# A third group of 256 tokens, fourteen whole seven-product groups, sums of g in three operations, and another order of the later steps

## The chip, the cores and the metric

The kernel runs on one core of a Trainium2 chip. The metric is the device time of one execution in microseconds (us). A core has five engines that each work through a queue of their own in order: TensorE (PE, with its weight loads PEld), VectorE (DVE), ScalarE (ACT), GpSimd (POOL) and SyncE (SP, which issues most DMAs).

## The reference, cut to what matters

```
a = softmax(phi, axis=2)                       # (8, 8, 576, 32)
k_m, v_m = a^T k, a^T v                        # (8, 8, 32, 64)
attn = softmax(scale * q k_m^T)                # (8, 8, 576, 32)
x = (attn v_m) as (4608, 512)                  # 8 batches of S = 576 tokens
h = x @ w_in                                   # w_in (512, 2048)
g = max(0.01 * h, h)
out = g @ w_out                                # w_out (2048, 512)
```

The inputs of the first part are float32, the weights come as 64-bit floats and are brought to float32 on the chip. What costs is the second part, two large products over 4608 tokens.

## The kernel before, in words

**Folding.** Attention ends in scores a of 32 memories per head, 256 values per token. v_m is folded into w_in once per batch b and quarter j of the 2048 hidden columns (`fold_products`, L1235, a step `W{b}{j}.p`; ACT writes the high half of the folded weights, L1268, steps `h0 h1`; DVE the low half, L1274, steps `l0 l1`). So h is a product over 256 values instead of 512.

**Precision.** Every factor is a pair of float16 halves, and a product is three matmuls: high by high, low by high, high by low.

**The older groups.** Tokens are taken in groups. Groups G = 0, 1 and 2 have 384 tokens each (batches 0 and 1, 1152 tokens). G = 0 is done in float32 while the weights still arrive. G = 1 and 2 go by units m of 256 hidden columns, eight a group: `P{m}.i` the up product (L1328, `up_products`, six matmuls for each 128 hidden columns), `V` the leaky activation on ACT (L1335), `C` the high half of g (`hi_old`, L1345, a copy on DVE), `L` the low half (`lo_old`, L1349, DVE), `O{m}.i` the down product (L1415): for each 128 hidden columns three tiles of 128 tokens, three matmuls of 512 columns each. `Z{G}.t` scales a tile on ACT and sends it with four DMAs on SP.

**The later groups.** Batches 2 to 7 (3456 tokens) go in 14 groups of 256 tokens, G = 3 to 16; the 14th has 128 tokens. A group has four steps k, one per quarter j (k = 0 to 55). `p{k}.i` is an up product of 128 hidden columns (L1457, `up_late`): six matmuls of 256 columns, or six and six of the two parts where a group crosses from one batch into the next. Two such products share one PSUM bank, a half each. `v{k}.i` is the activation (ACT, L1473). For a whole group the down product saves one product in eight: two tiles of tokens by two halves of the 512 output columns by two halves of the hidden columns need eight block products, and sums and differences of blocks make it seven, as Strassen and Winograd do. `s{k}` makes four sums of g blocks of 256 columns (`add_g`, L1494, four DVE operations), `c{k}.h` the high halves (ACT, L1498), `l{k}.h` the low halves (DVE, L1502), and `d{k}.n`, n = 0 to 6, the products (L1525, `down_late`): each six matmuls of 256 columns, into one half of four accumulator banks (one of its own, p1, and three pairs). The sums of w_out blocks are made once (`add_up`, L454). When a group's four k are done, `x{G}.p` copies p1 (ACT, L1535), `x{G}.0` to `x{G}.3` add the banks up (DVE, L1538, L1540, L1543, L1545), `z{G}.t` scales and sends. The 14th group, of one tile, has no blocks to add: its `d{k}.n`, n = 0 to 7, are plain products (`down_tile`, L1560, three matmuls of 256 columns each, 96 in all), and `store_half` (L1392 to L1403) sends the two halves of its tile.

**What sets the order.** Nothing is scheduled by the compiler: `OPENING` and `LATER` list some 2150 step names, and each engine takes its instructions in the order in which the steps stand there. The framework sets the semaphores: a step waits for what it reads, for the readers of what it overwrites, and a new accumulator takes a PSUM bank when one has been read out.

Of the kernel before, what the change touches and what calls it, by code (L numbers as in the profile page):

```python
# [1720 lines left out]
```

## Time and profile before

| what | value |
|---|---|
| median of 3 runs | 646.2 us (645.8 to 647.45) |
| the profiled execution's own time | 645.63 us |
| its span, first to last instruction | 643.9 us |
| granted TensorE clock | 1.000 of full speed |
| PE / DVE / ACT busy | 634.0 / 512.9 / 394.2 us |
| matmuls recorded | 7149 |

The profiled execution lies 0.57 us below the median of the runs. Busy time of an engine is the union of its instructions. A matmul's recorded duration contains its way through the array, so consecutive ones overlap: what a matmul costs in a row of them is the distance from one to the next, which the chain of waits gives where it lists a run of matmuls with its length and count.

### The profile page before, as it was taken

To read this page: it belongs to the slowest core of one execution; us is meant where nothing else is said; L and a number is where in the kernel's file an instruction comes from. 1 tells how busy PE (TensorE), PEld (TensorE's weight loads), DVE (VectorE), ACT (ScalarE), POOL (GpSimd) and SP (SyncE) were. 2 spreads that over 40 slices of the span, in tenths; PEclk is the share of its full clock that TensorE was granted. 3 is DMA by queue.
4 is the path that set the end of the run, shared out by engine and by line. 5 is a ranking of instruction groups with operands and counts; after the bars stand their busy time and mean duration, and the time that the engine had idled before them with its cause. 6 is when DMAs were issued, how large, how long until landed. Compare 5 with 4: busy or idle time off the path is not lost.

```text
span 643.9 us, 16869 instructions
## 1 busy us (share of the span) xinstructions
PE 634.0 (98%) x7149; PEld 481.7 (75%) x7149; DVE 512.9 (80%) x861; ACT 394.2 (61%) x683; POOL 30.0 (5%) x46
## 2 busy tenths in 40 slices
PE   8999999999999999999999999999999999999997
PEld 4544455665546788888888888887888888889896
DVE  5776899998987899899779865799887897574641
ACT  3898987764553556477556655656574576565553
POOL 0000121000010001002000010000010001000000
PEclk9999999999999999999999999999999999999999
DMA  9998732214502645501271001164114101010102
GB/s 324 337 380 275 247 110 50 83 21 91 198 10 33 133 152 84 180 32 42 33 193 70 13 22 43 23 124 148 35 27 82 26 19 33 3 34 1 35 2 50
DMA packets 85403, 61.14 MB, mean 95 GB/s; under 512 B 61648, under 2 KB 68560, under 8 KB 85328
## 3 DMA queue, kind: packets, MB, share of 16 engines
q1 hardware_dynamic: 84848, 59.64, 32.6%
q8 instruction: 56, 0.92, 0.6%
q10 hardware_dynamic: 480, 0.43, 0.2%
q14 instruction: 19, 0.16, 0.1%
HBM read 50.59 MB, written 9.45 MB: 93 GB/s over the span
## 4 chain that ended last, share of the span: by engine, by line
PE 93%; DVE 2%; DMA 2%; ACT 1%; SPq 1%; issue 1%; POOL 0%; DVEq 0%; ACTq 0%; POOLq 0%
PE po L1525 31%; PE ph L1457 22%; PE po L1415 15%; PE ph L1328 8%; PE ph L1525 5%; PE pa L1235 4%; PE pa L788 3%; PE po L1560 1%; DMA arena<-in_moe_w_out_dram 1%; PE po L1623 1%; PE pa L1038 1%; SPq L615 1%; DMA arena<-in_q_dram 0%; ACT wi L424 0%; PE pa L357 0%
## 5 line engine op out<-in xcount | busy, mean ns | idle before, releaser
L1525 PEld LDWEIGHTS <-arena 128*128 128x128 f16 x2184 | 210.2, 98 | 32.9 <-issue 10.0
L1473 ACT ACTIVATE wi<-ph,g_sc 128x256 f32<-128x256 f32 (+1 forms) x224 | 98.8, 464 | 162.0 <-PE ph L1457 153.9
L1457 PE MATMUL ph<-a,w_mem 128*128 128x256 f16 (+3 forms) x1440 | 144.8, 246 | 0.0
L1457 PEld LDWEIGHTS <-w_mem 128*128 128x128 f16 x1440 | 114.7, 98 | 13.6 <-issue 2.9
L1525 PE MATMUL po<-arena 128*128 128x256 f16 x936 | 122.0, 273 | 0.0
L1525 PE MATMUL po<-wo,arena 128*128 128x256 f16 x936 | 122.0, 273 | 0.0
L1415 PE MATMUL po<-wo,arena 128*128 128x512 f16 (+1 forms) x384 | 110.3, 433 | 0.0
L1502 DVE TENSOR_TENSOR arena<-arena 128x1024 f16<-128x1024 f32 x52 | 63.5, 1221 | 21.3 <-ACT arena L1498 21.2
L1502 DVE TENSOR_TENSOR arena<-wi,arena 128x768 f16<-128x768 f32 (+1 forms) x60 | 54.6, 910 | 10.1 <-ACT arena L1498 10.1
L1494 DVE TENSOR_TENSOR arena<-wi 128x256 f32<-128x256 f32 x104 | 40.4, 429 | 25.9 <-ACT wi L1473 25.3
L1498 ACT CAST arena<-arena 128x1024 f16<-128x1024 f32 x52 | 54.4, 1046 | 8.0 <-DVE arena L1494 7.7
L1328 PE MATMUL ph<-a,w_mem 128*128 128x192 f16 (+2 forms) x304 | 52.1, 317 | 0.0
L1415 PEld LDWEIGHTS <-arena 128*128 128x128 f16 x288 | 27.9, 98 | 29.6 <-issue 0.6
L1498 ACT CAST arena<-wi 128x768 f16<-128x768 f32 (+1 forms) x60 | 46.5, 776 | 1.5
L1494 DVE TENSOR_TENSOR arena<-wi,arena 128x256 f32<-128x256 f32 x104 | 45.6, 439 | 1.8
L1525 PE MATMUL ph<-wo,arena 128*128 128x256 f16 x312 | 42.6, 273 | 1.0 <-DVE t L1114 1.0
L1200 POOL TENSOR_TENSOR a<-t,a 128x128 f16<-128x128 f32 (+3 forms) x17 | 21.7, 1296 | 445.0 <-ACT a L1195 445.0
L1415 PEld LDWEIGHTS po<-wo,arena 128*128 128x128 f32 x96 | 17.7, 190 | 20.4 <-issue 17.9
L1235 PE MATMUL pa<-wi,vT 64*32 64x512 f16 (+1 forms) x704 | 29.6, 420 | 0.1
L1328 PEld LDWEIGHTS <-w_mem 128*128 128x128 f16 x240 | 20.8, 98 | 10.6 <-issue 3.9
L1335 ACT ACTIVATE arena<-ph,g_sc 128x384 f32<-128x384 f32 x32 | 18.3, 579 | 16.1 <-PE ph L1328 15.8
L1268 ACT ACTIVATE w_mem<-pa 128x512 f16<-128x512 f32 x40 | 22.7, 596 | 8.4 <-PE pa L1235 7.4
(236 smaller groups left out, 759.6 us busy)
## 6 DMA issues: line engine op xcount, KB each, us to landing
out_dram<-obs SPq DMA_DIRECT2D x140, 64.0 KB, 1.7
arena<-in_q_dram SPq DMA_DIRECT2D x96, 72.0 KB, 2.8
arena<-in_moe_w_in_dram SPq DMA_DIRECT2D x12, 512.0 KB, 7.1
arena<-in_moe_w_out_dram SPq DMA_DIRECT2D x8, 768.0 KB, 7.9
arena<-in_k_dram SPq DMA_DIRECT2D x5, 1152.0 KB, 5.5
arena<-in_v_dram SPq DMA_DIRECT2D x5, 1152.0 KB, 9.1
arena<-in_phi_dram SPq DMA_DIRECT2D x7, 576.0 KB, 4.6
arena<-in_k_dram SPq DMA_DIRECT2D x8, 288.0 KB, 4.9
```

Of the source, the lines that this page charges most:

```text
L788: nc.tensor.matmul(var["pk"][g][hh * M:(hh + 1) * M, cs], ld["phi"][rows, hh, j, :], ld["kv", hh][rows, kinds[0]:kinds[-1] + 1, j, :], sta ...
L1200: nc.gpsimd.tensor_tensor(piece(lo, tb), piece(t2, tb), piece(hi, tb), ALU.subtract)
L1235: nc.tensor.matmul(pf[g][cols, :], lhs, rhs, start=(n == 0), stop=(n == len(passes) - 1), tile_position=(g * D, hh * M),)
L1268: nc.scalar.activation(tiles(halves(w16(b, j), g)[:, 0]), w(g), AF.Copy, scale=ws)
L1328: nc.tensor.matmul(ph[:, t0:t0 + n * SB], lhs, rhs, start=(m == 0), stop=(m == len(seq) - 1))
L1415: nc.tensor.matmul(po, lhs, rhs, start=(f == 0 and m == 0), stop=(f == NQ * NF - 1 and m == len(seq) - 1),)
L1457: nc.tensor.matmul(ph[:, t0:t0 + n], lhs, rhs, start=(m == 0), stop=(m == len(seq) - 1))
L1473: nc.scalar.activation(dst, ph, AF.Prelu, scale=g_sc2[:, j:j + 1], alpha=SLOPE)
L1494: nc.vector.tensor_tensor(gt[:, x], y, z, op)
L1498: nc.scalar.copy(dst[:, 0], src)
L1502: nc.vector.tensor_tensor(dst[:, 1], src, dst[:, 0], ALU.subtract)
L1525: nc.tensor.matmul(acc, g[:, x, s, u], rhs, start=(h == 0 and j == 0 and u == 0 and m == 0), stop=(j == NQ - 1 and u == 1 and m == 2), ski ...
```

## The change

G = 2 shrinks from 384 to 256 tokens (768 to 1023), its tile count from three to two, so that the later groups start at token 1024 instead of 1152 and 14 whole groups of 256 reach 4608. `down_tile` and `store_half` go; the last group is combined and sent by new steps `end.*`. G = 2 now reads a block of 192 tokens and a third of another (64), each as its own matmuls; the first later group reads 128 tokens of batch 1 and 128 of batch 2, so batch 1's folded weights serve it too. The signs of some sums are turned (w_out blocks and g blocks alike), which lets one operation of 512 columns make two of the four sums of g; the odd hidden tiles' activation produces the value with the other sign. The high half of g in the older groups moves from DVE to ACT. `LATER` and the last part of `OPENING` are new orders, found by a search that took a PSUM bank as one thing; steps of different k now stand much more mixed. `w_turn`, the turn of the buffers for folded weights, changes with it.

```diff
-    NG2 = -(-((B - 2) * S) // (2 * HT))
+    GL = 2 * P
+    X0 = 2 * S - P
+    NG2 = (B * S - X0) // (2 * HT)
...
-    w_turn = iter([4, 5, 0, 1, 4, 2, 0, 3] + [4, 0, 1, 2, 6, 3] * B)
+    w_turn = iter([4, 5, 0, 1, 4, 2, 0, 3] + [4, 0, 6, 1, 2, 3] * B)
...
+    def width(G):
+        return GL if G == G2 - 1 else GT
...
+        for b, tb, c0, t0, n in spans(G * GT, width(G)):
...
-        nc.vector.tensor_copy(g[:, 0], gf_old(u))
+        nc.scalar.copy(g[:, 0], gf_old(G, u))
...
-            pos[G] = [ps_o.tile([P, E], F32, name="po") for t in range(NT)]
-        for t in range(NT):
+            pos[G] = [ps_o.tile([P, E], F32, name="po") for t in range(width(G) // P)]
+        for t in range(width(G) // P):
...
-        for x, y, z, op in (
-            (0, gf[:, 0], gf[:, 2], ALU.add), (3, gf[:, 1], gf[:, 0], ALU.subtract),
-            (1, gf[:, 1], gt[:, 0], ALU.subtract), (2, gf[:, 3], gt[:, 1], ALU.add),
-        ):
-            nc.vector.tensor_tensor(gt[:, x], y, z, op)
+        two = gf[:, 0:1].broadcast_to([P, 2, 2 * P])
+        nc.vector.tensor_tensor(gt[:, 0:2], two, gf[:, 1:3], ALU.subtract)
+        nc.vector.tensor_tensor(gt[:, 2], gf[:, 1], gt[:, 1], ALU.subtract)
+        nc.vector.tensor_tensor(gt[:, 3], gf[:, 3], gt[:, 2], ALU.subtract)
...
+    def combine_last(n):
...
+        dst, psum, by, add = {
+            0: (o[:, 1], pair[0][:, 1], minus, o[:, 0]),
+            1: (o[:, 2], pair[1][:, 0], sc, o[:, 1]),
+            3: (o[:, 1], pair[2][:, 0], minus, o[:, 1]),
+            4: (o[:, 2], pair[2][:, 1], minus, o[:, 2]),
+            5: (o[:, 0], pair[0][:, 0], minus, o[:, 0]),
+        }.get(n, (None,) * 4)
...
+            nc.vector.scalar_tensor_tensor(dst, psum, by, add, ALU.mult, ALU.add)
+
+    def send_last(x, n):
...
+        for y, (b, x0) in enumerate(columns(G, t)):
+            eng = nc.scalar if y % 2 else nc.sync
+            eng.dma_start(
+                rows[b, x0 // 32, :, cs], obs[32 * y:32 * y + 32, x * EH:(x + n) * EH]
+            )
...
-        for n in range(7 if whole(G2 + m // NQ) else 2 * NF):
+        for n in range(7):
```

The turn from one group to the next in the old `LATER`, after k = 39 (group G = 12; the other turns look much like it):

```
v41.1 d39.1 x12.p d39.2
p41.2 x12.0 d39.3 v41.2 c40.1 d39.4 x12.1 p41.3 x12.2 d39.5 l40.0 v41.3 d39.6 c41.0 p42.0 x12.3
p42.1 l40.1 v42.0 d40.0 v42.1 z12.0 d40.1 s41 z12.1 d40.2 p42.2 l41.0 d40.3 v42.2 c41.1 d40.4 p42.3
```

Two places of the new `LATER` that the prediction reads, the end of the group whose last step is k = 47 and the fold of batch 6's last quarter, and its last lines:

```
v49.0 d46.5 d45.3 d45.4 v49.1 p49.2 c48.0 p49.3 d47.0 l48.0 v49.3 d46.3 v49.2 s48 c48.1 d47.6 p50.1
p50.0 x14.p v50.0 d46.2 d46.4 d47.1 l48.1 v50.1 s49 c49.0 l49.0 z13.1 c49.1 p50.3 p50.2 d47.3 l49.1
d47.2 v50.2 v50.3 d48.0 p51.0 x14.0 p51.1 v51.0 d47.4 d47.5 x14.1 d48.3 d48.4 v51.1 p51.3 x14.2
x14.3 d48.1 s50 d48.5 v51.3 d48.6 c50.0 c50.1 p51.2 p52.1 v51.2 c51.0 d48.2 d49.0 z14.1 z14.0 l50.1
...
a7.Q0 l36.1 a7.D6 c37.0 p38.0 v38.0 a7.E1 s37 v38.1 l37.0 a7.E22 a7.E21 d35.5 p38.3 x11.0 c37.1
d36.0 x11.1 v38.3 W63.p x11.2 W63.h0 d35.6 p38.2 d36.3 d36.1 W63.h1 l37.1 W63.l0 v38.2 W63.l1 x11.3
p39.0 p39.1 v39.1 W70.p s38 v39.0 c38.0 W70.h0 l38.0 c38.1 d36.4 d36.5 p39.3 p39.2 l38.1 v39.2 d37.1
...
end.p d54.5 z15.0 d55.4 d55.2 end.0 d55.3 d55.5 end.1 end.2 d55.6 end.3 end.4 d53.1 end.z1 d54.1
end.z2 d55.1 end.5 end.z0
```

## Rows read from the trace of the kernel before

**Rows 1.** The page, busy time and share of each engine.
```profile
PE 634.0 (98%) x7149; PEld 481.7 (75%) x7149; DVE 512.9 (80%) x861; ACT 394.2 (61%) x683; POOL 30.0 (5%) x46
```

**Rows 2.** Busy time by stretch: length, then PE, PEld, DVE, ACT, POOL, PEclk, DMA.
```profile
40.00:98.00 58.00, 57.72 (x451) 28.23 (x450) 46.01 (x86) 50.75 (x79) 8.62 (x10) 1.00 0.69 230
98.00:225.00 127.00, 127.00 (x1234) 75.46 (x1233) 115.55 (x182) 74.35 (x126) 3.71 (x5) 1.00 0.33 78
225.00:330.00 105.00, 104.80 (x1425) 90.11 (x1423) 94.12 (x151) 62.09 (x111) 6.32 (x6) 1.00 0.36 88
330.00:440.00 110.00, 108.92 (x1491) 94.23 (x1489) 89.96 (x157) 64.62 (x115) 2.98 (x3) 1.00 0.27 74
440.00:560.00 120.00, 120.00 (x1362) 103.92 (x1360) 98.00 (x161) 72.67 (x126) 5.25 (x5) 1.00 0.18 41
560.00:639.74 79.74, 79.32 (x876) 70.92 (x873) 41.55 (x72) 42.91 (x83) 0.00 (x0) 1.00 0.09 21
639.74:643.90 4.16, 0.01 (x1) 0.00 (x0) 0.48 (x1) 0.00 (x0) 0.00 (x0) 1.00 0.25 63
```

**Rows 3.** Waits of PE behind 98 us: us in total, times, longest.
```profile
PE ph L1525 <- DVE t L1114: 1.0, 1, 1.0
PE ph L1457 <- ACT wi L1473: 0.4, 1, 0.4
```

**Rows 4.** The chain of waits: start us, length us, run of matmuls.
```profile
114.82 1.94 PE po L1415 x9
...
142.68 1.95 PE ph L1328 x12
...
341.29 1.34 PE ph L1457 x24
...
574.78 1.31 PE po L1525 x12
...
578.07 1.34 PE ph L1457 x24
```

**Rows 5.** Groups by shape inside the last two L1457 runs of rows 4.
```profile
L1457 PE MATMUL ph<-a,w_mem 128*128 128x192 f16 x12 | 1.3, 246 | 0.0
L1457 PE MATMUL ph<-a,w_mem 128*128 128x64 f16 x8 | 0.6, 193 | 0.0
...
L1457 PE MATMUL ph<-a,w_mem 128*128 128x128 f16 x21 | 1.3, 219 | 0.0
```

**Rows 6.** Groups by line and shape, DVE and ACT: count, busy us, mean ns.
```profile
L1345 DVE CAST arena<-arena 128x768 f16<-128x768 f32 x16 | 8.8, 550 | 2.2 <-ACT arena L1335 2.2
L1494 DVE TENSOR_TENSOR arena<-wi,arena 128x256 f32<-128x256 f32 x104 | 45.6, 439 | 1.8
L1545 DVE TENSOR_TENSOR obs<-po,obs 128x512 f32<-128x512 f32 x13 | 8.9, 686 | 0.9 <-PE po L1525 0.7
L1540 DVE TENSOR_TENSOR obs<-po,obs 128x256 f32<-128x256 f32 x13 | 5.5, 420 | 6.6 <-PE po L1525 6.5
L1502 DVE TENSOR_TENSOR arena<-arena 128x1024 f16<-128x1024 f32 x52 | 63.5, 1221 | 21.3 <-ACT arena L1498 21.2
L1502 DVE TENSOR_TENSOR arena<-wi,arena 128x768 f16<-128x768 f32 x52 | 51.2, 985 | 0.0
L1274 DVE SCALAR_TENSOR_TENSOR w_mem<-pa,w_mem 128x512 f16<-128x512 f32 x40 | 26.2, 678 | 0.3 <-ACT w_mem L1268 0.2
L1268 ACT ACTIVATE w_mem<-pa 128x512 f16<-128x512 f32 x40 | 22.7, 596 | 8.4 <-PE pa L1235 7.4
L1498 ACT CAST arena<-wi 128x768 f16<-128x768 f32 x52 | 43.3, 832 | 1.3
```

**Rows 7.** Timeline, the last computing instruction.
```profile
639.78 0.48 DVE L1396 TENSOR_SCALAR obs<-po,osc 128x256 f32<-128x256 f32 x1 [4.63 <-PE po L1560]
```

**Rows 8.** Timeline, the two up products p30.0, p30.1 and their activations.
```profile
445.67 1.47 PE L1457 MATMUL ph<-a,w_mem 128*128 128x256 f16 x12
...
447.18 0.84 ACT L1473 ACTIVATE wi<-ph,g_sc 128x256 f32<-128x256 f32 x2 [1.28 <-PE ph L1457]
```

More of the change, by code (lines that the diff above doesn't have):

```diff
@@ L299 @@
     pp_max = const.tile([P, 1], F32, name="pp_max")
-    g_sc = const.tile([P, NQ], F32, name="g_sc")
-    g_sc2 = const.tile([P, NQ], F32, name="g_sc2")
-    osc = const.tile([P, B], F32, name="osc")
-    osc_t = const.tile([P, B // 2], F32, name="osc_t")
+    g_scs = const.tile([P, 4 * NQ], F32, name="g_scs")
+    g_sc, g_sc2, g_sc2n = (g_scs[:, x * NQ:(x + 1) * NQ] for x in range(3))
+    scales = const.tile([P, 2 * B], F32, name="scales")
+    osc, osc_t = scales[:, 0:B], scales[:, B:B + B // 2]
+    osc_1, osc_n = (scales[:, x:x + 1] for x in (B + B // 2, B + B // 2 + 1))
     IO, LATE, SUMS, TMP, G_OLD, W_OLD, END = 6144, 23040, 8192, 47616, 51712, 70144, 75264
@@ L1297, in fold_scales, with spans @@
             )
-    def blocks(G):
-        return [(G // 3 * 2 + x // NB, x % NB) for x in range(G % 3 * 2, G % 3 * 2 + 2)]
+    def width(G):
+        return GL if G == G2 - 1 else GT
+    def spans(x, n):
+        res, t0 = [], 0
+        while t0 < n:
+            b, tb, c0 = (x + t0) // S, (x + t0) % S // SB, (x + t0) % SB
+            m = min(SB - c0, n - t0)
+            if m == SB and res and res[-1][0] == b and res[-1][4] % SB == 0:
+                res[-1][4] += m
+            else:
+                res.append([b, tb, c0, t0, m])
+            t0 += m
+        return res
     gs = {}
@@ L1371, in row_scale @@
         if bs[0] == bs[-1]:
-            return osc[:, bs[0]:bs[0] + 1]
+            return osc_1 if G >= G2 and bs[0] < FB else osc[:, bs[0]:bs[0] + 1]
         return osc_t[:, bs[0] // 2:bs[0] // 2 + 1]
@@ L1537, in combine @@
             p1 = o[:, 3:4].broadcast_to([P, 2, EH])
-            nc.vector.tensor_tensor(o[:, 0:2], pair[0], p1, ALU.add)
+            nc.vector.tensor_tensor(o[:, 0:2], p1, pair[0], ALU.subtract)
         elif n == 1:
@@ L1544, in combine @@
         else:
-            nc.vector.tensor_tensor(o[:, 1:3], pair[2], o[:, 1:3], ALU.add)
+            nc.vector.tensor_tensor(o[:, 1:3], o[:, 1:3], pair[2], ALU.subtract)
     def finish(G, t):
@@ L1632, in all_bounds @@
             out_scale(b)
+        nc.vector.tensor_scalar_mul(osc_1, osc[:, FB - 1:FB], 1.0 / G_SUMS)
     steps["e2."] = all_bounds
@@ L1653 @@
     for G in range(G2):
-        for t in range(NT):
+        for t in range(width(G) // P):
             steps[f"Z{G}.{t}"] = lambda G=G, t=t: store(G, t, pos[G][t])
@@ L1676 @@
             steps[f"z{G}.{t}"] = lambda G=G, t=t: finish(G, t)
-    G = G2 + NG2 - 1
-    for h in range(2):
-        steps[f"end.{h}"] = lambda h=h: store_half(G, h, pos[G][h])
+    for n in ("1", 0, 1, 2, 3, 4, 5):
+        steps[f"end.{'p' if n == '1' else n}"] = lambda n=n: combine_last(n)
+    for x, n in ((1, 1), (2, 2), (0, 1)):
+        steps[f"end.z{x}"] = lambda x=x, n=n: send_last(x, n)
     for b in range(B):
```

345 lines of the change are left out of this document (157 added, 188 removed).

## The prediction

> **What bounds the kernel now.** I read the busy shares first: PE is busy 98% of the span, DVE 80%, ACT 61% [rows 1]. A busy PE is not yet a PE that works at its pace, so the second view is busy time by stretch: from 98 us on, when the weights are in, PE lacks 0.20 + 1.08 + 0.42 = 1.70 us of 541.74 us, at a granted clock of 1.00 throughout (of 2.4 and 1.2 GHz, the upper level), while DVE and ACT have idle time in every stretch [rows 2]. The third is the list of PE's waits: two stand behind 98 us, of 1.0 us (turned scores of a late attention) and 0.4 us (an activation in the last, half group) [rows 3]. The last is the chain of waits, for the pace: in a run of matmuls nothing but columns costs time. 9 of 512 columns take 1.94 us, 0.2156 each; 12 of 384 take 1.95, 0.1625 each; 12 of 256 take 1.31, 0.1092 each [rows 4]. So the time is the number of matmul columns, and almost no wait is left that a better order could win: 1.7 us, and 0.28 us more between 40 and 98 us [rows 2].
>
> **The change part by part: PE.** All f16 matmuls of the changed groups, priced by the runs.
> - G = 2, up: 16 products of six matmuls of 384 columns, 96 x 0.1625 = 15.60 us. In their place stand 96 pairs of 192 and 64 columns. Such pairs stand in groups that cross a batch: 24 matmuls in 1.34 us, 12 pairs, 0.1117 a pair [rows 4, 5]. 96 x 0.1117 = 10.72. Difference -4.88.
> - G = 2, down: the third tile goes, 16 x 3 matmuls of 512 columns: 48 x 0.2156 = -10.35.
> - Last group, up: 96 matmuls of 128 columns become 96 of 256. 24 of 128 take 1.34 us, 0.0558 each [rows 4, 5]. 96 x (0.1092 - 0.0558) = +5.12.
> - Last group, down: 96 matmuls of 256 become 4 x 7 x 6 = 168: 72 x 0.1092 = +7.86.
> - The first later group crosses from batch 1 to batch 2: 192 of 128 columns for 96 of 256, 10.71 - 10.48 = +0.23. The other later groups cross as often as before.
>
> The sum is -2.02 us. Put otherwise, half a group goes from eight products to seven: 24 matmuls fewer, 2.62 us, less 0.6 for short pieces and roundings.
>
> **Short matmuls.** The 64-column pieces keep pace with their columns in the row: a pair takes hardly more than one matmul of 256 (0.1117 to 0.1092). The Trainium skill, TensorE: Matmul & The Clock Gate, section Back-to-back issue gap, speaks against the change here: it gives about 81 ns as the sustained distance of matmuls of 128 columns, weight load included, where this trace shows 56. By that page, with 64 columns no cheaper, the sum would be about +5 us, an estimate. The trace decides, and I keep 0.1117.
>
> **DVE and ACT.** `C` leaves DVE: 16 x 0.550 = -8.8. The four sums of `s{k}` took 4 x 0.439; now they are one of 512 columns (nearest row 0.686, a PSUM operand) and two of 256, 1.56 us in place of 1.76: 52 x 0.2 = -10.4. The last group gets four of them, +6.2, and its low halves grow from 8 x 0.439 to 4 x (1.221 + 0.985), +5.3 [rows 6]. DVE ends 8 us lighter of 513. ACT takes the copies, at most 16 x 0.832 = 13.3 us between 98 and 225 us, where it works 74 of 127 [rows 2, 6]. All of this costs nothing: PE's columns hide it, and without that cover the 13.3 us would be the price. Two small extra operations on scales (`g_sc2n`, `osc_1`) come before the first `V` of G = 1, not on PE's queue; each is bounded by a 256-column operation, 0.44.
>
> **The order.** Every step behind some 65 us has a new place, its DMAs included: loads of the later batches and sends of results share SP's queue, a send waits there for its scaling, and what stands behind it waits too. `Z2.2` takes four sends away, and the last group sends twelve DMAs for eight. The bounds: below, all waits go, -1.70 behind 98 us; above, each engine step that PE needs comes late. I take the waits as they are, except that 0.42 goes with the half group that held it, because 1.7 in 542 us is a rate that also a new order of the same kind can keep.
>
> **The end.** Last matmul, one DVE operation of 256 columns (0.48), four DMAs of 32 KB, 4.16 us in all [rows 2, 7]. After: `d55.1`, `end.5` (0.42 to 0.48 by the rows of its size), four such DMAs [rows 6, 7]. The sends `end.z1` and `end.z2` are issued one and two steps of 0.655 us earlier and delay the last by anything from nothing to two issues. Zero is taken.
>
> **Sum.** 645.63 - 2.02 - 0.42 = 643.19 on the profiled execution. The median of the runs lies 0.57 above that execution, so 643.8 us, 2.4 us or 0.37% below 646.2. A measurement tells about 0.3% of this kernel from no change, 1.94 us, so 644.3 is the line.
>
> **The rivals.**
> *The gain is eaten by shorter distances (same).* Between a product of PE and the step of PE that needs what ACT and DVE made of it, the list has some steps of other work. `W63.p` and `p39.0` had many; now four steps of 0.655, 2.62 us, stand there. ACT's high half and two of DVE's low halves in turn take 0.596 + 2 x 0.678 = 1.95, and `l37.1` (1.221) stands ahead of them on DVE [rows 6]: 3.17 if it starts late. `W22` and `W53` are as short. At the end of k = 47, `d47.4` and `d48.1` have four steps between them, and before such turns had about nine. Three folds and thirteen turns of banks that lose 0.1 to 0.2 us each cost some 2 us: 645.8. For: fewer steps of cover. Against: 2.62 us still exceed what stands in the chain.
>
> *A bank's turn stops PE at each group end (slower).* PE may not write a bank's other half while ACT or DVE reads one half: p30.0's activation starts at 447.18, only when both products p30.0 and p30.1 have left PE at 447.14 [rows 8]. The Trainium skill, PSUM — Partial Sum Buffer, section PSUM bank collisions raise a hardware error, states such a dependency for any two engines on one bank, and the trace agrees. At a turn DVE must add up with 0.420 and 0.686 [rows 6] before the new group's accumulators have a bank; if DVE comes to it one operation of 0.686 too late at each of 13 turns, it costs 8.9 us: 652.7. It makes the kernel slower from (2.4 + 1.94) / 13 = 0.33 us a turn. For: turns of four steps. Against: DVE gets lighter, and where most turns lie it has 10.9 of 105 to 22 of 120 us free [rows 2].
>
> *The new order also removes the other waits (faster).* A further 0.20 + 1.08 of idle PE [rows 2, 3] gone: 642.5. More can't come from waits behind 98 us.
>
> *Short matmuls cost more than their columns.* If each piece of 64 or 128 columns took what 256 take, the pairs would be 96 x 0.2184, +5.4 in place of -4.88, the last group's up 0, the split +10.5: the sum -10.35 + 7.86 + 5.4 + 10.5 = +13.4 and the time 659.2. Rows 4 and 5 speak against it outright.
>
> *The change doesn't do what it says.* If the new last group kept eight products, 24 matmuls more, 2.62 us, leave 646.4. The list of steps has 28 `d` for it, so hardly.
>
> **How the numbers follow.** The sum with waits as they are, 0.38; the other waits gone too, 0.15; gain eaten, 0.30; banks' turns, 0.13; short matmuls 0.01; not as said 0.03. Faster: 0.38 + 0.15, less 0.01 of the first that lies past the line, 0.52; same: 0.30 + 0.03 + 0.01 = 0.34; slower: 0.13 + 0.01 = 0.14. The range: below, all waits gone (642.5), and 1.1 us more for the spread of the runs shown (1.65 from lowest to highest): 641.4. Above, half of the turns' price on the forecast, 643.8 + 4.5 = 648.3; the worse half of that case, the short matmuls and a little below stay outside, under 2 in 10. The forecast's own range is 642.9 to 644.4.
>
> **What would show it.** Right: 24 matmuls of 256 columns' worth fewer; runs at the same pace (0.109, 0.2156); a pair of 192 and 64 in G = 2 at 0.112; 16 `C` on ACT, DVE some 8 us lighter; PE's idle time behind 98 us at 1 to 2 us. Wrong: PE waits on L1538 to L1545 or on L1274 that sum to more than 2 us, or PE waiting before `co.1` or the first `V` of G = 1, because the last lines of the opening moved. A longer tail than 4.2 us would be the end's mistake.

## The result, and the profile after

The changed kernel takes 652.8 us (median of 6 runs, 650.3 to 654.7) where the kernel before takes 645.2 in the same sessions: a ratio of 1.0113, 95% interval 1.0092 to 1.0133. It is slower by some 7 us; the prediction had it faster, at 643.8 us, and its range, 641.4 to 648.3, does not hold the time. The profiled execution took 651.47 us, span 649.7. Three of the other five executions, 652.7 to 654.7 us, had a mean granted TensorE clock of 0.996 or 0.997 where the profiled one has 1.000, so the 1.3 us from it to the median can't be read from the profile.

The page's first part (busy time, share of the span, instructions), to be held against [rows 1]:

```profile
PE 632.1 (97%) x7365; PEld 490.1 (75%) x7365; DVE 519.9 (80%) x813; ACT 400.0 (62%) x698; POOL 31.2 (5%) x46
```

PE is busy 1.9 us less, which is what the change was reckoned to save, and the span is 5.8 us longer. So PE stands still more. Busy time by stretch of the changed kernel (columns as in [rows 2]; the last two stretches end at the last matmul and at the end of the span):

```profile
40.00:98.00 58.00, 56.70 (x446) 27.20 (x444) 44.98 (x88) 49.40 (x77) 6.84 (x8) 1.00 0.69 229
98.00:163.00 65.00, 63.73 (x644) 39.61 (x645) 64.26 (x89) 49.92 (x84) 2.60 (x3) 1.00 0.26 59
163.00:225.00 62.00, 58.30 (x829) 40.93 (x828) 49.65 (x82) 35.94 (x70) 3.32 (x3) 1.00 0.39 99
225.00:255.00 30.00, 27.62 (x389) 23.46 (x387) 29.55 (x41) 17.29 (x32) 2.92 (x4) 1.00 0.49 123
255.00:330.00 75.00, 75.00 (x1057) 64.03 (x1055) 68.49 (x103) 42.98 (x79) 2.79 (x3) 1.00 0.30 75
330.00:440.00 110.00, 110.00 (x1338) 95.50 (x1338) 86.00 (x137) 62.80 (x114) 2.62 (x2) 1.00 0.30 82
440.00:560.00 120.00, 119.20 (x1543) 103.80 (x1528) 97.34 (x146) 72.04 (x131) 7.05 (x5) 1.00 0.14 29
560.00:645.26 85.26, 85.26 (x828) 76.72 (x826) 51.99 (x76) 42.24 (x74) 0.00 (x0) 1.00 0.09 21
645.26:649.70 4.44, 0.00 (x0) 0.00 (x0) 0.48 (x1) 0.00 (x0) 0.00 (x0) 1.00 0.40 103
```

Subtract the second number of each row from the first. From 40 us to the last matmul PE lacks 1.30 + 1.27 + 3.70 + 2.38 + 0.80 = 9.45 us; by [rows 2] it lacked 1.98 before. Nearly all of it lies before 255 us; behind 255 the new order stands still 0.80 us in 390. The balance is: columns -1.9, waits +7.5, the end 4.44 for 4.16, +0.3; the span grew by 5.8.

PE's waits behind 40 us (in all, times, longest), to be held against the two of [rows 3]:

```profile
PE po L1516 <- DVE obs L1536: 1.8, 1, 1.8
PE ph L1453 <- DVE w_mem L1279: 1.5, 1, 1.5
PE pa L793 <- issue: 1.4, 2, 0.8
PE po L1516 <- ACT obs L1399: 1.3, 1, 1.3
PE ph L1341 <- DVE arena L1279: 1.1, 1, 1.1
PE po L1412 <- DVE arena L1364: 0.9, 1, 0.9
PE pa L793 <- DVE w_mem L1279: 0.6, 1, 0.6
PE pa L361 <- DVE t L1119: 0.6, 1, 0.6
```

Seven waits behind another engine, each once: at 97, 127, 155, 184, 186, 208 and 251 us; and two in which PE waits for nothing that the profile shows. Three of the seven have a transfer behind them: those at 184 and 186 us share one, and the one at 208 has its own. SP's queue of the changed kernel (start, length, instruction):

```profile
165.88 0.40 SPq L590 DMA_DIRECT2D arena<-in_k_dram  x1
166.38 0.45 SPq L590 DMA_DIRECT2D arena<-in_v_dram  x1
166.93 0.46 SPq L679 DMA_DIRECT2D d_mx<-mx  x1
176.04 1.14 SPq L683 DMA_DIRECT2D r1k<-d_mx  x2
```

The fourth instruction reads back what the third wrote and is held until that has landed: a write of 2 KB takes 9.1 us, with two loads of 1152 KB each gone out 0.5 and 1.0 us ahead of it (e2_kv shows that they are the cause). DVE pays for it, and then for something else (timelines of DVE and of POOL):

```profile
179.61 0.39 DVE L691 TENSOR_TENSOR r1k<-r1k 128x128 f32<-128x128 f32 x1 [3.98 <-DMA r1k<-d_mx]
...
182.24 2.62 DVE L1364 TENSOR_TENSOR arena<-arena 128x512 f16<-128x512 f32 x1
```

```profile
181.86 3.28 POOL L1205 TENSOR_TENSOR a<-t,a 128x1024 f16<-128x1024 f32 x2 [59.77 <-ACT a L1200]
```

The 128x512 low half took 2.62 us. It ends 0.55 us behind the end of the first of POOL's two subtractions, 184.31: it seems to have stood while POOL worked (e6_s08 takes POOL away). The waits at 184 and 186 stand behind these two. At 251 us it is the same picture, here in the timelines of DVE and of POOL:

```profile
249.34 0.69 DVE L1483 TENSOR_TENSOR arena<-wi 128x512 f32<-128x512 f32 x1
250.07 2.23 DVE L1484 TENSOR_TENSOR arena<-wi,arena 128x256 f32<-128x256 f32 x1
```

```profile
249.74 2.85 POOL L1205 TENSOR_TENSOR a<-t,a 128x1024 f16<-128x1024 f32 x2 [64.56 <-ACT a L1200]
```

An operation of 0.43 us took 2.23, and `x3.3` (L1536), for which PE waits 1.78, comes two operations later. The Trainium skill, SBUF — State Buffer, section Who interferes with whom, says that a VectorE instruction with two inputs in SBUF contends with a GpSimd instruction that reads SBUF, and that the pair of ports which they share is an exclusive lock; the trace agrees, with 2.62 and 2.23 us.

At 208 us the second transfer: four sends go out behind 16 loads of q, the last of the four at 204.38 us, and land 4.5 us later; ACT's scaling of the next tile waits for them, and PE for ACT (timelines of SP, ACT and PE):

```profile
202.95 8.29 SPq L1395 DMA_DIRECT2D out_dram<-obs  x7
209.13 0.69 ACT L1399 ACTIVATE obs<-po,scales 128x512 f32<-128x512 f32 x1 [2.64 <-DMA out_dram<-obs]
209.87 1.36 PE L1516 MATMUL po<-wo,arena 128*128 128x256 f16 x11 [1.28 <-ACT obs L1399]
```

The other places, at 97, 127 and 155 us, are plain lateness in a full queue. Between 98 and 163 us DVE works 64.26 of 65 us; before it worked this much (columns: length, DVE busy, PEclk, DMA share, GB/s):

```profile
98.00:163.00 65.00, 60.76 (x90) 1.00 0.27 62
```

It is the order that fills this stretch and not the new sums of g, the first of which runs at 194 us. Ten copies `C`, 5.5 us, have left it; in their place stand, among others, four operations of the attention that the old order ran ahead of it or behind it (L655, L1141, L1144, L1171: 5.8 us), and two low halves of folded weights took 1.40 us each beside POOL's subtractions, at 119.9 and 121.2, in place of 0.75.

### The profile page after: what moved, and what is told of

The parts are those of the page before. It is cut to its first block, busy times and chain, and to the rows that moved or that the text cites. A ratio compares the mean times of both kernels' runs of the same rounds, so it can differ in the third digit from the quotient of the medians.

```text
span 649.7 us, 17275 instructions
## 1 busy us (share of the span) xinstructions
PE 632.1 (97%) x7365; PEld 490.1 (75%) x7365; DVE 519.9 (80%) x813; ACT 400.0 (62%) x698; POOL 31.2 (5%) x46
## 3 DMA queue, kind: packets, MB, share of 16 engines
HBM read 50.59 MB, written 9.45 MB: 92 GB/s over the span
## 4 chain that ended last, share of the span: by engine, by line
PE 73%; DVE 12%; DMA 8%; SPq 3%; issue 1%; ACT 1%; DVEq 0%; ACTq 0%
PE po L1516 34%; PE ph L1453 22%; PE ph L1516 6%; PE po L1412 3%; PE pa L1240 3%; PE pa L793 3%; DMA arena<-in_moe_w_in_dram 2%; SPq L620 2%; DMA arena<-in_q_dram 2%; DVE w_mem L1279 2%; DMA d_mx<-mx 1%; DVE arena L1364 1%; DVE wi L438 1%; PE ph L1341 1%; DVE r1k L655 1%
## 5 line engine op out<-in xcount | busy, mean ns | idle before, releaser
L1516 PEld LDWEIGHTS <-arena 128*128 128x128 f16 x2352 | 226.6, 98 | 37.1 <-issue 11.4
L1516 PE MATMUL po<-arena 128*128 128x256 f16 x1008 | 128.9, 273 | 1.8 <-DVE obs L1536 1.8
L1516 PE MATMUL po<-wo,arena 128*128 128x256 f16 x1008 | 128.9, 273 | 1.3 <-ACT obs L1399 1.3
L1453 PEld LDWEIGHTS <-w_mem 128*128 128x128 f16 x1512 | 119.0, 98 | 14.2 <-issue 2.9
L1467 ACT ACTIVATE wi<-ph,g_scs 128x256 f32<-128x256 f32 x112 | 52.8, 472 | 93.8 <-PE ph L1453 88.0
L1412 PE MATMUL po<-wo,arena 128*128 128x512 f16 (+1 forms) x336 | 99.9, 441 | 0.9 <-DVE arena L1364 0.9
L1469 ACT ACTIVATE wi<-ph,g_scs 128x256 f32<-128x256 f32 x112 | 52.8, 471 | 71.9 <-PE ph L1453 68.8
L1493 DVE TENSOR_TENSOR arena<-wi,arena 128x768 f16<-128x768 f32 x56 | 53.1, 947 | 16.6 <-ACT arena L1489 16.4
L1489 ACT CAST arena<-wi 128x768 f16<-128x768 f32 x56 | 46.6, 832 | 1.5 <-PE po L1516 1.0
L1412 PEld LDWEIGHTS <-arena 128*128 128x128 f16 x240 | 22.3, 98 | 24.5 <-DVE arena L1364 1.4
L1483 DVE TENSOR_TENSOR arena<-wi 128x512 f32<-128x512 f32 x56 | 38.3, 684 | 2.5 <-ACT wi L1469 1.8
L1279 DVE SCALAR_TENSOR_TENSOR w_mem<-pa,w_mem 128x512 f16<-128x512 f32 x40 | 26.8, 681 | 10.6 <-ACT w_mem L1273 7.5
L1341 PEld LDWEIGHTS <-w_mem 128*128 128x128 f16 x312 | 23.1, 98 | 6.8 <-issue 3.9
```

Of the source, the lines that this page charges most:

```text
L1279: nc.vector.scalar_tensor_tensor(tiles(t[:, 1]), w(g), ws, tiles(t[:, 0]), ALU.mult, ALU.subtract)
L1341: nc.tensor.matmul(ph[:, t0:t0 + n], lhs, rhs, start=(m == 0), stop=(m == len(seq) - 1))
L1412: nc.tensor.matmul(po, lhs, rhs, start=(f == 0 and m == 0), stop=(f == NQ * NF - 1 and m == len(seq) - 1),)
L1453: nc.tensor.matmul(ph[:, t0:t0 + n], lhs, rhs, start=(m == 0), stop=(m == len(seq) - 1))
L1467: nc.scalar.activation(dst, ph, AF.Prelu, scale=g_sc2n[:, j:j + 1], alpha=1.0 / SLOPE)
L1469: nc.scalar.activation(dst, ph, AF.Prelu, scale=g_sc2[:, j:j + 1], alpha=SLOPE)
```

## The experiments

Theory A: each wait has its own cause in the order of some steps and goes when they are moved. Theory B: DVE carries too much, and a wait that is taken away comes back further on. Theory C: the new arithmetic costs the time. Theories D, E and F come with the expectations that name them. In the lists of steps `a{b}` is a step of the attention of block b, `i{j}.k` and `i{j}.l` the high (ACT) and low (DVE) halves of a quarter of w_in, `o{j}` the same for w_out, with its sums `o{j}.s` (DVE) and their halves `o{j}.m` (ACT) and `o{j}.n` (DVE). Lines of steps in the diffs are cut to what moves, and of many moves some are left out. Each ratio is to the kernel before in the same session. Times of PE are taken from 40 us to the last matmul, by the view of busy time in a window; they are those of the one profiled execution, which can lie 1 to 2 us from the median (651.33 us for e10_send, 655.33 for e3_turn, 645.89 for e14_both).

| kernel | us | ratio, 95% interval | PE busy | PE idle |
|---|---|---|---|---|
| before | 645.2 to 646.1 | 1 | 597.76 | 1.99 |
| changed | 652.81 | 1.0113 (1.0092 to 1.0133) | 595.82 | 9.44 |
| e1_same | 653.08 | 1.0132 (1.0105 to 1.0158) | 596.22 | 10.48 |
| e2_kv | 651.06 | 1.0085 (1.0067 to 1.0103) | 596.95 | 7.40 |
| e3_turn | 654.01 | 1.0130 (1.0109 to 1.0151) | 598.92 | 10.14 |
| e4_all | 646.68 | 1.0021 (1.0004 to 1.0038) | 595.47 | 5.03 |
| e5_round2 | 646.26 | 1.0017 (1.0004 to 1.0030) | 595.33 | 5.32 |
| e6_s08 | 654.97 | 1.0144 (1.0117 to 1.0170) | 596.85 | 10.59 |
| e7_both | 652.57 | 1.0109 (1.0086 to 1.0131) | 597.44 | 8.91 |
| e8_mirror | 645.53 | 1.0000 (0.9986 to 1.0014) | 597.84 | 3.00 |
| e9_due | 649.51 | 1.0047 (1.0031 to 1.0063) | 596.75 | 5.76 |
| e10_send | 650.20 | 1.0059 (1.0040 to 1.0079) | 596.15 | 8.93 |
| e11_w10 | 651.49 | 1.0076 (1.0050 to 1.0103) | 595.91 | 8.97 |
| e12_last | 645.83 | 1.0006 (0.9995 to 1.0017) | 595.67 | 3.97 |
| e13_page | 655.90 | 1.0159 (1.0134 to 1.0185) | 596.02 | 12.81 |
| e14_both | 647.66 | 1.0027 (1.0013 to 1.0041) | 595.47 | 4.33 |
| e15_more | 646.81 | 1.0012 (0.9999 to 1.0025) | 595.73 | 4.17 |

**e1_same**, no edit.

> The changed kernel once more, with only the line breaks of its step lists moved, as the measure for the next three on the same chip. All theories: 1.010 to 1.014 of the kernel before. PE waits behind 96 us at the same seven places (1.1, 0.6, 0.6, 0.9, 1.5, 1.3 and 1.8 us in the profile of the change), 7.7 us in all, if they belong to the order and not to the one profiled execution.

The same seven places, within 2 us of their old times, and 653.08 us. So they belong to the program and not to one execution.

**e2_kv**, one transfer ahead of two others:

```diff
-P21.1 a3.kv L19
+P21.1 a3.A4 a3.kv L19
...
-W21.p a3.A4 V21.0
+W21.p V21.0
```

> One step moved: the round trip of batch 3's maxima through DRAM (a3.A4) is issued ahead of batch 3's k and v loads instead of behind them. Theory A (each wait of PE has its own cause in the order and comes back alone): the 2 KB write lands in under 2 us instead of 9.1, VectorE's 4.0 us wait for the read-back goes, and with it the two PE waits of 0.9 and 1.5 us near 184 and 186 us: 2 to 2.7 us faster than the same run of the changed kernel, 0.997 of it. Theory B (VectorE has too much to do between 83 and 187 us, and a wait removed at one place comes back at the next): under 1 us. Theory C (the new arithmetic costs the time, its short matmuls and operations): no change.

2.0 us back. SP's queue of this kernel:

```profile
166.35 0.37 SPq L677 DMA_DIRECT2D d_mx<-mx  x1
168.73 1.14 SPq L681 DMA_DIRECT2D r1k<-d_mx  x2
169.96 0.54 SPq L588 DMA_DIRECT2D arena<-in_k_dram  x1
```

The write lands in 2.4 us, DVE no longer waits for it, and PE has no wait left between 163 and 200 us. The 2 us are shown to come from the order of three transfers. The same three stand in the bad order once more, at 337 to 347 us, in the changed kernel and in this one (the write takes 8.7 and 8.9 us), and PE waits for nothing there: the slow write cost time only where DVE stood waiting for it.

**e3_turn**, one operation ahead of the three sums it waited behind:

```diff
-a3.S07 s6 d5.0 x3.3 a4.D3
+a3.S07 x3.3 s6 d5.0 a4.D3
```

> One step moved: the last addition of a group's banks (x3.3) stands ahead of the next sums of g (s6) on VectorE instead of behind them, one of which took 2.23 us in place of 0.43 beside a GpSimd operation. Theory A: the PE wait of 1.8 us near 252 us goes, nothing else changes: 1.5 to 2 us faster than the changed kernel. Theory B: this place lies behind the overloaded stretch, so it may go too, at most 1.8. Theory C: no change.

The wait at 251 is gone, and 1.4 us stand at 258 in its place, an up product behind an activation (L1451 behind L1465): here theory B. What was moved was the victim; POOL's subtraction still held DVE for its 2 us. PE's busy time is 2.7 us over that of e1_same since the granted clock of this execution was 0.50 from 189.7 to 193.1 and from 213.6 to 217.0 us, behind waits of 1.92 and 2.17 us; two other executions, at a mean clock of 1.000, took 652.7 and 653.2 us, as e1_same did.

**e4_all**, these two moves and five more:

```diff
-W00.l1 a2.A4
+W00.l1 W10.l0 a2.A4
...
-L11 P13.0 W13.h1 a2.kv2 W13.l0 V13.1 o1.l2 o1.s3 W13.l1 a2.C10
+L11 P13.0 W13.h1 a2.kv2 W13.l0 V13.1 W13.l1 o1.l2 o1.s3 a2.C10
...
-a2.C4 a3.A1 L15
+a2.C4 a2.E1 a3.A1 L15 a2.E21
...
-a3.B20 o3.n1 O20.1
+a3.B20 W20.l0 o3.n1 Z1.0 O20.1
```

> Seven such moves together, one or two for each of the seven places: W10.l0 ahead of the scales, W13.l1 ahead of a weight half, a2.E1 and a2.E21 ahead of weight halves, a3.A4 ahead of a3.kv, W20.l0 ahead of sums of w_out, Z1.0 ahead of the loads of q, x3.3 ahead of s6. Theory A: the sum of the waits, 7.7 to 8.7 us, comes back; the kernel is within 1 us of 644, that is 0.995 to 1.000 of the kernel before, and what the matmul columns save (2.0 us) shows for the first time. Theory B: at most 3 us come back, 1.007 or more. Theory C: 1.010 or more.

6.4 us back of 7.4, by moves alone: all products and all sums are as in the changed kernel, so theory C falls for these 6.4, and PE's busy time agrees (595.47). But the ratio, 1.0021, lies above theory A's range and below theory B's. What PE still waits for:

```profile
PE pa L790 <- issue: 1.8, 2, 1.2
PE ph L1450 <- ACT wi L1464: 1.2, 1, 1.2
PE ph L1338 <- ACT arena L1345: 0.8, 1, 0.8
PE pa L790 <- DVE w_mem L1276: 0.6, 1, 0.6
PE pa L1040 <- DVE t L1116: 0.4, 1, 0.4
```

**e5_round2**, moves at the second to fifth of these:

```diff
-W02.h1 o1.k0 Z0.0 W11.l0 o0.l1 V9.1
+W02.h1 V9.1 o1.k0 Z0.0 W11.l0 o0.l1
...
-o1.l1 o1.n1 O10.0 L11 P13.0 W13.h1 a2.kv2 W13.l0
+o1.l1 W13.l0 o1.n1 O10.0 L11 P13.0 W13.h1 a2.kv2
...
-a2.E1 a3.A1 L15 a2.E21
+a2.E1 L15 a2.E21 a2.E22 a3.A1
...
-c6.1 c6.0 p7.3 p7.2 v7.2 d5.6 a4.Q0 l6.1 v7.3
+p7.3 p7.2 v7.2 v7.3 c6.1 c6.0 d5.6 a4.Q0 l6.1
```

> The order with the seven moves, and four more moves at the waits that were left in it: the activation V9.1 ahead of a store's copy, W13.l0 ahead of o1.n1, the 2.2 us reduction a3.A1 behind a2.E21 and a2.E22, and v7.2 and v7.3 ahead of c6.1 and c6.0. Theory A (each wait has its own cause in the order): the waits of 1.00 us at 108, 0.61 us at 155 and 1.34 us at 249 go and the one at 128 loses some 0.3 us: 642.8 to 644.8 us, ratio 0.995 to 0.9985 to the kernel before. Theory B (VectorE and ScalarE are so full that a wait that is taken away comes back at the next place): 645.5 to 648 us, with new waits of the same sum a few us further on.

Theory B: the waits at 108, 155 and 249 are gone and the one at 128 with them, and PE stands as long as before, 5.32 us to 5.03, now 0.3 at 110, 1.5 at 136 (`O12.0` behind `o2.l0`), 0.4 at 162, 1.4 at 252 to 254. Neither theory alone holds over both runs: e4_all won most of the waits back, and here, in a stretch where DVE hardly rests, a move shifts the wait.

**e6_s08** and **e7_both**, the subtraction of step S08 on DVE in every block, in the changed kernel and in e5's order:

```diff
-                    nc.gpsimd.tensor_tensor(
+                    nc.vector.tensor_tensor(
```

> The changed kernel with one edit: the subtraction of step S08 runs on VectorE in place of GpSimd. Theory D (a VectorE operation with two inputs stands still while GpSimd reads): the operations of 2.2 to 2.6 us beside it are back at 0.43 to 0.95 us, the wait of 1.95 us at 252 goes and the two at 184 and 186 shrink by up to 1 us together, since their other cause, the wait of 4 us for a transfer, stays: 649.5 to 651.5 us. Rival (VectorE pays as much for the subtraction as it stood still): 652.5 to 654 us, the same places.

> The eleven moves and S08 on VectorE together. Theory D: the same as the eleven moves alone or up to 1 us less, 642.3 to 644.5 us, since the moves have taken away most of the waits behind GpSimd's operation already. Rival (VectorE's added work delays what stands behind it): 0.5 to 2 us more than the eleven moves alone.

The mechanism is shown, the gain is not. DVE's timeline of e6_s08, at the place of the 2.23 us above:

```profile
249.58 0.42 DVE L1482 TENSOR_TENSOR arena<-wi,arena 128x256 f32<-128x256 f32 x1
250.04 0.42 DVE L1483 TENSOR_TENSOR arena<-wi,arena 128x256 f32<-128x256 f32 x1
```

0.42 us, as where POOL is idle, and the 128x512 low half at 183 takes 0.69 in place of 2.62. But POOL had made the subtraction ahead of its place on DVE's queue; there it now comes behind two low halves, and `p8.0` waits for it, 2.8 us in e6_s08 and 3.8 in e7_both. Both times, 654.97 and 652.57 us, lie above what either theory gave, and neither named this wait.

**e8_mirror**, in the kernel before, a3.kv moved to stand just ahead of a3.A4.

> The kernel before, with one move: the loads of k and v for block a3 issue just ahead of the small write of a3.A4, as they do in the changed kernel. Theory A: the small write lands 7 to 8 us after its issue in place of 1.4, VectorE waits 3 to 5 us for it near 196 us where it now waits for none, and TensorE loses 2 to 5 us at the packed products behind it: 647.5 to 650.5 us. Theory C (the changed kernel's time comes from its new arithmetic, not from the order of a few steps): 645 to 646.3 us.

645.5, as the kernel before; but the run does not test what it was for. SP had nothing to wait for ahead of the loads and sent them at 168.7 us (161.7 in the kernel before), still 20 us ahead of the write, which landed in 1.4 us. Moving a step in the list did not bring the two transfers together. Whether the old kernel would pay the same for that pair stays open.

**e9_due**, e5's order with work that is not yet due moved back, and four other moves, of which the diff shows one:

```diff
-C15 i2.k0 o3.l0
+C15 o3.l0
...
-a2.E1 L15 a2.E21 a2.E22 a3.A1 i1.k2
+a2.E1 L15 i1.l0 i2.k0 a2.E21 a2.E22 a3.A1 i1.l1 i2.k1 i1.k2
...
-v8.1 a4.E1 v8.0 s7 a4.E22 p8.2 a4.E21 d6.2
+v8.1 v8.0 s7 p8.2 a4.E1 a4.E22 a4.E21 d6.2
```

> The eleven moves, and seven more: three splits of weight pieces (i1.l0, i1.l1 and their successors on ScalarE i2.k0, i2.k1) later, since their products stand 25 us behind them, o2.l0 and l6.0 earlier, the store Z0.1 earlier, a4.E1 two places later on TensorE. Theory E (VectorE has no idle time from 96 to 152 us, so that there a wait is moved by an edit and not removed; only work that is not due can give the time back): the waits of 0.25 us at 110, 1.53 us at 136, 0.8 and 0.6 us at 252 to 254 go, 642.8 to 644.8 us, ratio 0.995 to 0.9985. Rival (every order of this kind has some 4 us of such waits, whatever is moved): 645.5 to 647 us.

649.5 us, above both forecasts. The waits named are gone or below 0.1 us, save 0.9 at 254, and the move made a worse one: ACT's activations V16.0 and V16.1 stood behind `i2.k0`, which waits for `i1.l0`. ACT and PE in their timelines, and PE's stretches behind it (length, busy PE, PEld, DVE, ACT, POOL, PEclk, DMA share, GB/s):

```profile
151.64 2.37 ACT L430 ACTIVATE wi<-wi,sw 128x768 f16<-128x768 f32 x3 [5.90 <-DVE wi L435]
153.92 0.81 ACT L1345 ACTIVATE arena<-ph,g_scs 128x256 f32<-128x256 f32 x2
```

```profile
154.43 0.85 PE L1338 MATMUL ph<-a,arena 128*128 128x192 f16 x12 [3.40 <-ACT arena L1345]
155.09 3.79 PE L1409 MATMUL po<-wo,arena 128*128 128x512 f16 x9
```

```profile
154.40:155.00 0.60, 0.57 (x9) 0.57 (x9) 0.60 (x1) 0.60 (x2) 0.00 (x0) 1.00 0.00 0
156.00:157.00 1.00, 1.00 (x4) 0.38 (x3) 1.00 (x2) 0.97 (x2) 0.00 (x0) 0.50 0.00 0
158.50:161.00 2.50, 2.50 (x29) 1.72 (x28) 1.11 (x3) 0.83 (x2) 0.00 (x0) 1.00 0.00 0
```

PE had stood 3.4 us; the granted clock fell to the lower level, 1.2 GHz, from 155 to 158.5, and 9 matmuls of 512 columns took 3.79 us where they take 1.94 [rows 4]. So the mistake cost 3.4 + 1.8 us.

**e10_send** and **e11_w10**, single moves of e4_all in the changed kernel, one where DVE has idle time and one where it has none:

```diff
-o3.n1 O20.1
+o3.n1 Z1.0 O20.1
```

```diff
-W00.l1 a2.A4
+W00.l1 W10.l0 a2.A4
```

> The changed kernel with one move: the store step Z1.0 ahead of O20.1, before the loads of q. Its place lies where VectorE has idle time. Theories A and E: the wait of 1.5 to 2.6 us at 208 goes and nothing takes its place, 650.5 to 651.8 us. Rival (also here the wait moves on): 652.5 to 654 us.

> The changed kernel with one move: W10.l0 ahead of the 1.45 us operation of co.4. Its place lies in the stretch where VectorE has no idle time. Theory E: the wait of 1.3 us at 97 goes and comes back within 15 us (the kernel with seven moves has 1.0 us at 108 that the changed kernel has not), 652.3 to 653.8 us. Theory A (each wait by itself): 651.3 to 652.1 us.

e10_send: no wait between 200 and 225 us, 650.2 us, 2.6 below the changed kernel and 2.9 below e1_same. Its profile shows only 0.5 and 1.6 us less idle PE than theirs, with 0.7 us more at 155 and some 0.4 more at 184 in an execution that took 651.33; so 2 to 3 us is what the times say, and no count of waits confirms it. e11_w10: the wait at 97 is gone and 0.9 us stand at 108 (L1338 behind L1345), as theory E has it; the time, 651.5 (650.65 to 653.1), is what theory A gave and can't tell them apart by itself.

**e12_last**, both faults of e9_due mended:

```diff
-L15 i1.l0 i2.k0 a2.E21 a2.E22 a3.A1 i1.l1 i2.k1 i1.k2 i1.l2 V16.0 o3.s2 V16.1 P17.1
+L15 i1.l0 a2.E21 a2.E22 a3.A1 i1.l1 i1.k2 i1.l2 V16.0 o3.s2 V16.1 i2.k0 P17.1
...
-x3.2 c5.0 v6.3
+x3.2 c5.0 a3.S07 v6.3
...
-a3.S07 x3.3 s6 d5.0
+x3.3 s6 a3.S08 d5.0
...
-                    nc.gpsimd.tensor_tensor(
+                    (nc.vector if b == 3 else nc.gpsimd).tensor_tensor(
```

> The eighteen moves with the two places mended that lost time in them: i2.k0 and i2.k1 behind V16.1 and V17.1 on ScalarE, so that the wait of 3.4 us at 154 and the low clock behind it go, and at 249 to 255 the subtraction S08 of block a3 on VectorE behind s6, with l6.1 and l6.0 ahead of a4.Q0 and a4.E1 behind p8.3, so that s6 does not stand still beside GpSimd and the wait of 1.0 us at 254 goes. Theory E (the loss is in which step stands ahead of which on a full VectorE): 642.8 to 644.8 us, ratio 0.995 to 0.9985, faster than both kernels. Rival (every order of this kind has some 4 us of such waits, whatever is moved): 645.5 to 648 us.

The best order found: 645.8 us, no difference from the kernel before (1.0006), which is what the rival gave and not theory E. The wait of 3.4 us is gone, and of the other 0.3 is left. PE idles 3.97 us, and is busy 595.67, 2.1 us less than before: the columns that the change takes away are there, and waits have eaten them.

**e13_page**, **e14_both** and **e15_more** ask for PE's waits without a cause. In all twelve profiles of the new order up to here they stand at the same two places of PE's stream, counted over matmuls, weight loads and the semaphore instructions between them: its instructions 5057 and 10945 (in some profiles one more), 23 x 256 apart. Two packs go later:

```diff
-v6.0 a4.C10 p6.2 a4.C2 W31.l0 a4.C30 c4.1 v6.2 d3.4 d2.5 l4.1 d4.0 p7.0
+v6.0 p6.2 W31.l0 c4.1 v6.2 d3.4 d2.5 l4.1 d4.0 a4.C10 a4.C2 p7.0
...
-a7.C10 s33 d32.0
+s33 d32.0
...
-d32.1 l33.1 a7.C30 p34.3 a7.C31
+d32.1 a7.C10 a7.C2 l33.1 p34.3
```

> The changed kernel with two moves on TensorE: the packs of 144 short products a4.C10 and a7.C10, each with what hangs on it, go four steps (some 96 instructions) later. In every run of the new order so far TensorE waits for nothing that the profile shows at the same two places of its stream, its instructions 5057 and 10945, for 0.36 to 1.21 us each; both lie 256 instructions behind another such boundary inside the same pack, which runs through 288 instructions in 2.25 us. Theory F (the wait belongs to the place in the instruction stream: a second block of 256 instructions is wanted before it has come): both gaps shrink to 0.2 us or less, since the pack then holds one boundary only; 651.3 to 652.3 us, against 653.1 measured for the changed kernel. Rival (it belongs to the packs or to what stands about them): gaps of 0.4 to 1.2 us stay in the same two packs, 652.5 to 654 us.

> The order of the last run with the same two moves of the packs. Theory F: its two gaps of 0.59 and 0.87 us go to 0.2 or less, 644.3 to 645.2 us, ratio 0.997 to 0.9995. Rival: as the last run, 645.5 to 646.3 us.

> The same with six moves more at the waits that the last order still had: o3.k2 and o3.l2 ahead of i1.l1 (O15.1 waited 1.05 us for o3.l2 at 157), a2.S01 and i2.l0 later (the store Z1.2 waited for o3.n3 at 161), x4.3 ahead of a5.A3 (1.2 us of waits at 280). Theory E: these waits go, 642.2 to 643.8 us, ratio 0.994 to 0.997, faster than both kernels: the columns that the change takes away are then seen. Rival (some 4 us of waits stay in every order): 644.5 to 646.3 us.

Theory F is right about the gaps. The pack a7.C10 in the changed kernel, its end from 469 us on, and in e13_page:

```profile
468.75 1.16 PE L793 MATMUL pa<-arena 64*32 64x128 f32 x61
470.71 0.44 PE L793 MATMUL pa<-arena 64*32 64x128 f32 x12 [0.80 <-issue]
```

```profile
473.98 2.25 PE L791 MATMUL pa<-arena 64*32 64x128 f32 x144
```

Moved, it runs in 2.25 us for 3.40, without a stop; a4.C10 likewise, in 2.35 for 3.19. The other five packs of 144 hold one such place each, and none of them shows the wait in any run. It fits what the Trainium skill, Runtime: NRT & Kernel Launch, section Instruction fetch mechanics, says of a sequencer that refills its instructions in blocks of 256 by a DMA of its own; that this is mostly hidden, as the page adds, does not hold for two blocks in 2.25 us. But the time got no better, and all three times (655.9, 647.7 and 646.8 us) lie above both of their forecasts. PE waits elsewhere instead: in e13_page 1.4 us at 238, for an activation ahead of the moved pack, 1.5 at 260, for a late transposition of the same block, and 0.9 at 490; in e14_both 0.9 at 233, 0.9 at 242 and 0.5 at 481. The further six moves of e15_more (o3.k2 and o3.l2 behind a3.A1, i2.l0 behind L16, a2.S01 behind o3.n3, x4.3 ahead of a5.A3) took away the wait at 157 (those at 280 were already gone in e14_both), and 0.5 came at 165: 646.8 us, 1.0012 (0.9999 to 1.0025), no difference from the kernel before.

## Why the prediction was wrong

- **PE's columns: right.** The sum was -2.02 us; PE's busy time fell by 1.94 (597.76 to 595.82), and by 2.1 in the order with the fewest waits. Short matmuls keep pace: twelve matmuls of G = 2, six pairs of 192 and 64 columns, take 0.67 us at 192.74, 0.112 a pair. The third tile and the 24 matmuls are gone.
- **The 0.42 us of the half group: right.** From 560 us to the last matmul PE now lacks nothing.
- **The step that failed: "I take the waits as they are ... because 1.7 in 542 us is a rate that also a new order of the same kind can keep."** From 40 us on PE's idle time went from 1.98 to 9.45 us. The low rate belonged to that one list of steps and did not pass to the next: moving eight of 2167 steps took away 4.4 to 5.5 us of it (5.03 us left, of the 9.44 and 10.48 in the two profiles of the changed kernel).
- **The place was named wrong too.** The rivals looked for loss at the short folds `W22`, `W53`, `W63.p` and at thirteen turns between groups. Behind 255 us, where twelve of those turns and two of these folds lie, PE lacks 0.80 us, less than before. One turn, at 251, costs 1.8, and its cause is not a turn four steps short, but POOL's subtraction beside DVE. The loss is between 96 and 253 us, in the opening of the new order, where the weights' splits, the attention of the second and third block and G = 1 fall together. The view of busy time showed DVE at 115.55 of 127 us there [rows 2] and the prediction took from it that DVE has "idle time in every stretch"; over 98 to 163 alone it was 60.76 of 65, and the new order has 64.26.
- **A sign of being wrong that was named did come:** PE's waits behind the banks' additions and the folded weights' low halves (L1536 and L1279; L1545 and L1274 before) sum to 5.0 us, over the 2 us that the prediction set.
- **DVE 8 us lighter: wrong.** The page has 512.9 and 519.9. `C` left as reckoned; the sums did not get lighter. Of the two forms of the old 256-column operation the step took one mean, 439 ns, four times. The groups by line, before (with the busy time of all of L1494, over the whole span, behind it) and after:

```profile
L1494 DVE TENSOR_TENSOR arena<-wi 128x256 f32<-128x256 f32 x104 | 40.4, 429 | 25.9 <-ACT wi L1473 25.3
```

```profile
0.00:644.00 644.00, 81.71 (x208) 1.00 0.33 95
```

```profile
L1483 DVE TENSOR_TENSOR arena<-wi 128x512 f32<-128x512 f32 x56 | 38.3, 684 | 2.5 <-ACT wi L1469 1.8 <-ACT wi L1467 0.2
L1485 DVE TENSOR_TENSOR arena<-wi,arena 128x256 f32<-128x256 f32 x56 | 25.7, 460 | 2.0
L1484 DVE TENSOR_TENSOR arena<-wi,arena 128x256 f32<-128x256 f32 x56 | 25.6, 457 | 1.9
```

  104 operations of 429 ns and 104 of 439 [rows 6] are 90.3 us, but DVE was busy 81.7 with them: neighbours overlap. The new sums, three lines that do not overlap each other, hold it 89.6. So the old sums took 1.57 us a step k and not 1.76, the new ones take 1.60, and where the prediction had -4.2 us the runs have +7.9. That is 12.1 of the 14.7 us between the forecast of -7.7 and the measured +7.0. The mean duration of an operation is not what it takes of its engine, and here fewer, longer operations gave back the overlap.
- **ACT, +13.3 us at most, at no cost: half right.** ACT has 5.8 us more. Where PE waited for ACT, ACT had waited for a transfer (the store at 208) or for DVE.
- **The end, zero for bounds of up to two issues: nearly.** 4.44 us for 4.16.
- **"The gain is eaten by shorter distances", 645.8**, came nearest in kind: more waits behind late steps. Its sum was too small by 7 us, since it counted three folds and thirteen turns and none of the transfers, of POOL, or of the stretch before 255 us.
- **"A bank's turn stops PE at each group end"**, 652.7, meets the measured 652.8, but by luck: it had 0.69 us at each of thirteen turns, and twelve of the thirteen cost nothing to speak of.

What the seven waits were, as far as runs show it: 2.0 us two loads sent ahead of a small write (e2_kv), some 2 to 3 us, by the times, four sends behind the loads of q (e10_send); the rest is lateness on a DVE without rest, between 96 and 163 us, and around 250 us beside POOL, which one move or a few shift (e3_turn, e5_round2, e11_w10) and only several together take away (e4_all, e12_last). 1.4 us are the two places in PE's stream (e13_page), beside the seven. Whether some order of the new products beats the kernel before stays open: none of the orders tried did, and after e12_last the waits taken away brought others of about their sum (3.97, 4.33 and 4.17 us of idle PE). Most of what the change adds to DVE, 7.0 us in the changed kernel, stands in all of these orders, and no run took it out.

## What to carry to other kernels

When a change makes a program search its order anew, price the order and not only the products: the waits of the old one are no forecast for the new one, and here most of them came where an engine that feeds PE works through a whole stretch without rest. Read such a stretch in pieces of its own, not averaged with its neighbours, and look on the queues for small transfers that the path needs behind large ones that nobody waits for yet. In repair, move work that is not due away from the full engine; moving the victim ahead passed the wait on here.

## What was not expected of the hardware

- A DVE operation beside a subtraction on POOL took 2.23 to 2.62 us in place of 0.43 to 0.69, in both kernels (before: 2.25 at 243); the same subtraction took DVE 1.22 us and POOL 2.1 to 2.9.
- A write of 2 KB issued 0.5 us behind 2.3 MB of loads landed after 9.1 us, and after 2.4 issued ahead of them.
- After PE had stood 3.4 us (e9_due) the granted clock was at its lower level for 3.4 us. In e6_s08 and e7_both the same followed waits of 2.8 and 3.8 us (granted clock 0.56 from 257.3 to 259.7, and 0.50 from 256 to 258.5), so a long wait can cost more than its length. It does not always: waits of 2.1 us in e2_kv and of 1.92 and 2.17 in e3_turn were followed by such a stretch, one of 2.40 in e1_same and one of 2.15 in e13_page were not.
- PE stopped for 0.4 to 1.2 us in a pack of 144 short matmuls where its stream passed two boundaries of 256 instructions in 2.25 us, at the same instruction in all twelve profiles, and not where a pack held one boundary.
